# Attention, a Fourier mix and a feed-forward on one core: clears moved from the start into the first batch, mask rows loaded ahead of the identity, kept columns copied after the second stage, and the first batch's rows of maxima copied from POOL's queue

## The chip, the cores and the metric

One core of a Trainium2 chip. Its engines run side by side, each through its own instructions in order: TensorE (PE, with its weight loads PEld), VectorE (DVE), ScalarE (ACT), GpSimd (POOL) and SyncE (SP), which here only issues transfers. ACT and POOL issue transfers too, and all transfers run on the core's 16 DMA engines. The metric is device time in microseconds (us) of one execution; lower is better.

## The reference, cut to what matters

Attention over 8 batches of 8 heads, 576 positions of 64 numbers, with a mask in blocks of 64; then a real part of a two-dimensional Fourier transform of each batch's 576 x 512 result, a normalization, and a feed-forward of 512 to 2048 to 512.

```
scores = scale * np.matmul(q, k.transpose(0, 1, 3, 2))
scores = np.where(mask, scores, -1000000000.0)
scores = scores - np.max(scores, axis=-1, keepdims=True)
attn = np.exp(scores)
attn = attn / (np.sum(attn, axis=-1, keepdims=True) + 1e-09)
x = np.matmul(attn, v)            # heads side by side: (8, 576, 512)
X = np.fft.fft(np.fft.fft(x, axis=1), axis=2)
u = x + np.real(X)
un = (u - mu) / np.sqrt(var + 1e-06)
return u + np.maximum(un @ w_ch1, 0.0) @ w_ch2
```

## The kernel before

**Precision.** Products are made of two halves, a rounded high part and the rest as a low part, so most matmuls come in threes: high by high, low by high, high by low. The names show it: `ph` and `pl` are the two halves of the probabilities `p`, `VH` and `VL` of the values, `uh`/`ul` of the normalized rows, `gh`/`gl` of the hidden layer. POOL makes `pl` from `p` and `ph`, for every piece of every head.

**One head.** `lead` holds queries and keys' high parts, nine further rows for the mask, and `rest` the low parts; both are filled by copies on the chip. PE makes the maxima (`max_part`, four pieces, matmuls of `lead` alone with 72 rows), DVE reduces them into `M`, PE turns `M` by `ident` (`shift`), ACT makes the row `mt` from it, and a DMA puts `mt` into the last row of `lead`. Only then can PE make the head's `scores` (four pieces; the matmul of `lead` with 73 rows needs that row). ACT evacuates each piece twice (`ph` and `p`), POOL makes `pl`, and PE makes the values (`values`, 45 matmuls into `av`), which DVE divides by the sums. With each pair of heads the result goes to DRAM (`xd`).

**One batch.** After eight heads `mirror` reads `xd` back in two orders, into tiles and into `X2`, `U2` for the odd rows. DVE and ACT fold them (`folded`), `stage1` multiplies with tables `dft`, `stage2_sin` and `stage2_cos` do the other direction. A few columns of `stage1`'s result of two batches are kept in `ZP` (`zpc`, `zps`) and `ZTP` (`ztp`), 33 or 32 columns for each batch, since their rows are done for two batches together: `second_stage(2)` reads them after every odd batch. Rows and columns that nobody writes must be zero; that is what the clears are for. Then come the normalization and the feed (`first`, `second`; matmuls `h<-uh,W` and `acc<-W,gh`): two feeds for each batch and one more for every four batches.

**Weights.** 18 loads of 1 or 0.5 MB bring the feed's weights, issued by ACT (`weight_load`); DVE takes each apart in three passes, ACT squares it for a scale (`left`), and the first layer's low halves are made on PE (`W<-W,turns`) after the first batch's attention.

**What sets the order.** Each engine's order is written once, ahead of the run, by a planner. Work is cut into `Step`s with a chain of costs such as `("A0.26", "B", "Q0.6", "M0.05", "L1.6")`: A, D, G stand for time on ACT, DVE and POOL, P for POOL issuing a transfer, Q for SP issuing one, M for the transfer, L for its latency, B frees a PSUM bank. A step has keys that it waits for and a `place`, about the number of the head. From these the planner books queues, and takes the step that is ready with the lowest place; feed matmuls fill in where no other step is ready. A changed cost of one step so moves many instructions after it. DMA issues stand in the order of the engine that issues them.

**Lines that the change touches.** Line 255: the load of `ident`, POOL's first transfer. Lines 307 to 326: clears of `MAIN`, `DIAG` (start values of maxima), `X2`, `U2` on POOL, the loads of the masks' nine rows into the two `lead` tiles of heads 0 and 1 behind them, and clears of `ZTP` and `ZP` on DVE. `shift`: the copy of `mt` by SP. `stage1` and `stage1_tail`: ACT's copies of the kept columns at their ends. `table_lane`: four loads of `dft` by POOL, after heads 1, 2, 4 and 5.

Of the kernel before, what the change touches and what calls it, by code (L numbers as in the profile page):

```python
# [9 lines left out]
F32 = mybir.dt.float32  # L10
# [3 lines left out]
AF = mybir.ActivationFunctionType  # L14
# [18 lines left out]
HF = 2  # L33
# [186 lines left out]
def tile_attn_fourier_ffn(  # L220
# [31 lines left out]


    ident_r = const.tile([P, P], F32R, name="ident")
    gpsimd.dma_start(ident_r, c_id)
    ident = ident_r.bitcast(F32)
    rows = const.tile([P, 3], I32, name="rows")
    sync.dma_start(rows, c_rows)
# [32 lines left out]
    def both(h):  # L291

        return half_tiles(h % NB)[0:2]
# [10 lines left out]
    VH = [const.tile([P, 5, 2, D + 1], F16, name=f"VH_{i}") for i in range(2)]  # L304
    VL = [const.tile([P, 5, 2, D], F16, name=f"VL_{i}") for i in range(2)]
    ZT = const.tile([P, NCOS], F32R, name="ZT")
    for i in range(2):
        gpsimd.memset(MAIN[i], LEAST)
        gpsimd.memset(MAIN[i][0:64, 0:1], 0.0)
        gpsimd.memset(DIAG[i], LEAST)  # L310
    X2, U2 = (const.tile([P, DM], F32, name=x) for x in ("X2", "U2"))
    gpsimd.memset(X2, 0.0)
    gpsimd.memset(U2, 0.0)
    ZP = {(name, m): const.tile([P, 2, width], F32R, name=f"zp{name}{m}") for name, width in (("c", 98), ("s", 96)) for m in range(2)}
    ZTP = const.tile([P, 98], F32R, name="ztp")
    for i in range(HF):
        gpsimd.dma_start(LEAD[i][D:KS], c_masks)
        vector.tensor_scalar(LEAD[i][0:D, 0:64], ones[0:D, 0:64], 0.0, None, op0=ALU.mult)
    for i in range(2):
        vector.memset(VH[i][:, 0:4, :, D:D + 1], 1.0)  # L320
        vector.memset(VH[i][0:64, 4, :, D:D + 1], 0.0)
        vector.memset(VH[i][64:128, 4, :, D:D + 1], 1.0)
    vector.tensor_scalar(ZTP, ones[:, 0:98], 0.0, None, op0=ALU.mult)
    for t in ZP.values():
        for x in range(2):
            vector.tensor_scalar(t[:, x], ones[:, 0:t.shape[2]], 0.0, None, op0=ALU.mult)
    for at in range(0, NCOS, P):
        w = min(P, NCOS - at)
        vector.tensor_scalar(ZT[:, at:at + w], ones[:, 0:w], 0.0, None, op0=ALU.mult)
# [387 lines left out]
    def shift(h):  # L717

        t = ps_tile()
        mm(t[0:5, 0:P], M[h % 4][:, 0:5], ident_r, start=True, stop=True)  # L720
        yield
        if h >= HF:
            mt = work.tile([5, P], F32, name="mt", bufs=2).bitcast(F16)[:, 0:P]
            c = 2.0 ** -15
            scalar.activation(mt, t[0:5, 0:P], AF.Copy, bias=float(8.0 * PSHIFT * np.log(2.0)) * c, scale=-c)
            yield
            sync.dma_start(both(h)[0][KM:KS, 0:640].rearrange("r (j p) -> r j p", j=5), mt)
            yield
            return
        mt = work.tile([5, P], F32R, name="mt", bufs=2)  # L730
        scalar.activation(mt, t[0:5, 0:P], AF.Copy, bias=float(8.0 * PSHIFT * np.log(2.0)), scale=-1.0)
        yield
        dst = LEAD[h % NB][KM:KS, 0:640].rearrange("r (j p) -> r j p", j=5)
        sync.dma_start(dst.bitcast(F32), mt.bitcast(F32))
        yield

    probs = {}
# [102 lines left out]
    def max_lane():  # L840
        for h in range(2 * GP):
            for n in range(4):
                yield Step(
                    lambda n=n: max_part(h, n), 0.03 + sum(x[2] - x[1] for x in MAXPARTS[n]) / 2400.0, (f"D{(0.65, 0.49, 0.63, 0.93)[n]}",),
                    (("T", h),), ("M", h) if n == 3 else None, True, place=h - 0.6,
                )
            yield Step(lambda: shift(h), 0.12, ("A0.26", "B", "Q0.6", "M0.05", "L1.6"), (("M", h),), ("X", h), True, place=h - 0.6)
        for g in range(GP, B * H // 2):
            for n in range(4):
                d = f"D{(0.78, 0.42, 0.56, 0.91)[n]}"  # L850
                yield Step(
                    lambda n=n: pair_max(g, n), 0.06 + sum(x[2] - x[1] for x in PAIRPARTS[n]) / 2400.0, (d, "B", d),
                    (("hi", g),), ("M", 2 * g) if n == 3 else None, 2, place=2 * g - 1.6,
                )
            for h in (2 * g, 2 * g + 1):
                yield Step(
                    lambda: shift(h), 0.12, ("A0.26", "B", "Q0.6", "M0.05", "L1.6"), (("M", 2 * g), ("T", h)), ("X", h), True, place=h - 0.6
                )

    def value_lane():  # L860
# [12 lines left out]
    def fourier_steps(b):  # L873
# [69 lines left out]
        def stage1(name, m):  # L943
            mat, stack, k2, n = MATS[name]
            f0, f1, f2 = (fs[name, c] for c in range(3))
            ds = slice(P * m, P * (m + 1))
            t = ps_tile()
            i = 0
            for c, f in enumerate((f0, f1)):
                for a, w in ((0, 0), (1, 0), (0, 1)):  # L950
                    mm(t[:, 0:n], f[:, a, ds], mat[:, c, w], start=(i == 0), stop=False)
                    i += 1
            mm(t[:, 0:n], f2[0:k2, ds], stack[0:k2], start=False, stop=True)
            yield
            zz = z[name, m] = ztile(name, m).rearrange("p (x n) -> p x n", x=2)
            scalar.copy(zz[:, 0], t[:, 0:n])
            yield
            vector.tensor_tensor(zz[:, 1], t[:, 0:n], zz[:, 0].bitcast(F32), op=ALU.subtract)
            yield
            w = 33 if name == "c" else 32  # L960
            scalar.copy(ZP[name, m][:, :, o:o + w], zz[:, :, 256:256 + w].bitcast(F32))
            yield

        def stage1_tail():
            mat, stack, k2, n = MATS["c"]
            f0, f1, f2 = (fs["c", c] for c in range(3))
            t = ps_tile()
            i = 0
            for c, f in enumerate((f0, f1)):
                for w in range(2):  # L970
                    mm(t[0:2, 0:n], f[:, :, LDH], mat[:, c, w], start=(i == 0), stop=False, skip_group_check=True)
                    i += 1
            mm(t[0:1, 0:n], f2[0:k2, LDH:LDH + 1], stack[0:k2], start=False, stop=True, skip_group_check=True)
            yield
            scalar.copy(ZT[0:2], t[0:2, 0:n])
            yield
            vector.tensor_tensor(ZT[32:34], t[0:2, 0:n], ZT[0:2].bitcast(F32), op=ALU.subtract)
            yield
            scalar.copy(ZTP[:, o:o + 33], ZT[:, 256:289].bitcast(F32))
            yield  # L980

        bss = {}
# [4 lines left out]
        def stage2_sin(c):  # L987
            n = 128 if c < 2 else 96
            t = ps_tile()
            i = 0  # L990
            ns = slice(P * c, P * c + n)
            for m in range(2):
                for a, w in ((0, 0), (0, 1), (1, 0)):
                    lhs = z["s", m][:, a, ns] if c < 2 else last("s", m, a)
                    mm(t[0:n, 0:KCOL], lhs, sd[:, m, w], start=(i == 0), stop=(i == 5))
                    i += 1
            yield
            bs = bss[c] = work.tile([P, KCOL], F32, name="bs", bufs=1)
            if c == 2:
                gpsimd.memset(bs[96:97], 0.0)  # L1000
            scalar.copy(bs[0:n], t[0:n, 0:KCOL])
            yield

        def stage2_cos(c):
# [27 lines left out]
        D_ = lambda *a: ("d", b) + a  # L1032
        place = H * (b + 0.9)
        yield Step(
            mirror, 0.0, ("L3.0", "P3", "L2.5"), (("V", H * b + H - 1, 4),) + ((("F", feed_number(b - 2, 1)),) if b > 1 else ()), D_("u"),
            place=place,
        )
        def folds(name, op, width):
# [6 lines left out]
        def stages(name):  # L1045
            for m in range(2):
                yield Step(
                    lambda m=m: stage1(name, m), 0.87, ("A0.42", "D0.47", "A0.25"), (D_("f" + name),),
                    D_("z" + name) if m == 1 else None, True, place=place,
                )  # L1050
            if name == "c":
                yield Step(stage1_tail, 0.62, ("A0.4", "D0.46", "A0.23"), (D_("fc"),), D_("zt"), True, place=place)

        cos, sin = ("c", ALU.add, 257), ("s", ALU.subtract, 256)
        order = (folds(*cos), folds(*sin), stages("c"), stages("s"))
        for steps in order:
            yield from steps
        def second_stage(c):
            yield Step(lambda: stage2_sin(c), 0.67, ("A0.38",), (D_("zs"),), D_("b", c), True, place=place)
            yield Step(  # L1060
                lambda: stage2_cos(c), 0.78, ("D0.86", "B", "G3.0"), (D_("zc"), D_("zt"), D_("b", c)) + ((("F", feed_number(3, 2)),) if c == 2 and b == 5 else ()), D_("u", c), True,
                place=place,
            )

        for c in range(2):
            yield from second_stage(c)
        uu = tuple(D_("u", c) for c in range(3))
        yield from normalized_steps(low, uu[0:2], (store(b, 0), store(b, 1)), place)
        if b % 2:
# [84 lines left out]
    def feed_number(b, i):  # L1154

        return 2 * b + 1 + b // 4 + i
# [435 lines left out]
    def load_table(i):  # L1592
# [5 lines left out]
        gpsimd.dma_start(dft[:, lo:hi], c_dft[:, lo:hi])  # L1598
        yield

    def table_lane():
        for i in range(4):
            yield Step(lambda: load_table(i), 0.0, ("D0.15", "P1.0", "M2.3"), (("V", TABLES[i], 4),), ("dft", i), place=TABLES[i])

    def transform_lane():
# [114 lines left out]
```

## Time and profile before

| | us |
|---|---|
| median of 3 runs (1205.13 to 1212.7) | 1207.31 |
| the profiled execution | 1204.48 |
| its span, first to last instruction | 1202.3 |

Mean granted PE clock over the span: 0.965. By 40 slices of the span, each digit tenths:

```profile
PE   4767799998789999999999999999999999999998
PEclk9956989999889999999999999999999999999999
DMA  9687233443444234543435422360122021011100
```

A slice is 30 us. PE's row is busy share, the next its granted clock, the third the DMA engines' busy share. The first batch's attention takes the first three slices; from the 13th on PE is full.

How to read the rows of the next parts. A row of the order of time starts with its start and its length in us, then the engine, the line (L213 and L246 are helpers that record nearly every operation, so names of tiles tell more than lines), the operation, out<-in with tile names without numbers, the shape, xN where N equal ones were merged, and in brackets the idle time of its engine just before it and what ended that. SPq, ACTq are the issuing side of SP and ACT; a transfer that POOL issues is shown under POOL. Of DMA queues, q1 is SP's, q10 ACT's and q0 POOL's; a row has packets, MB and the time that the packets took as a share of 16 engines in the stretch asked for. A transfer's row shows when it was issued, not when it landed; landing is seen where somebody waits for it, or in the queue's row of a stretch.

### The profile page before, as it was taken

To read this page: it belongs to the slowest core of one execution; us is meant where nothing else is said; L and a number is where in the kernel's file an instruction comes from. 1 tells how busy PE (TensorE), PEld (TensorE's weight loads), DVE (VectorE), ACT (ScalarE), POOL (GpSimd) and SP (SyncE) were. 2 spreads that over 40 slices of the span, in tenths; PEclk is the share of its full clock that TensorE was granted. 3 is DMA by queue.
4 is the path that set the end of the run, shared out by engine and by line. 5 is a ranking of instruction groups with operands and counts; after the bars stand their busy time and mean duration, and the time that the engine had idled before them with its cause. 6 is when DMAs were issued, how large, how long until landed. Compare 5 with 4: busy or idle time off the path is not lost.

```text
span 1202.3 us, 26143 instructions
## 1 busy us (share of the span) xinstructions
PE 1122.9 (93%) x10182; PEld 824.4 (69%) x10182; DVE 741.8 (62%) x1616; ACT 630.8 (52%) x1374; POOL 475.6 (40%) x621
## 2 busy tenths in 40 slices
PE   4767799998789999999999999999999999999998
PEld 3544475675566777777776767677766766888875
DVE  6886876557857576666665566666656434454431
ACT  5666759757756566556574654675222212334320
POOL 4552414544653254425442533353334210455410
PEclk9956989999889999999999999999999999999999
DMA  9687233443444234543435422360122021011100
GB/s 259 194 253 233 105 106 87 121 124 103 123 115 103 76 87 106 113 132 81 123 99 142 126 82 82 91 151 14 32 43 56 23 60 30 28 36 26 28 19 18
DMA packets 94049, 115.07 MB, mean 96 GB/s; under 512 B 37591, under 2 KB 64129, under 8 KB 93926
## 3 DMA queue, kind: packets, MB, share of 16 engines
q1 hardware_dynamic: 86582, 89.06, 28.2%
q10 hardware_dynamic: 4384, 16.78, 4.3%
q0 software_dynamic: 2960, 7.58, 2.3%
q8 instruction: 80, 1.31, 0.5%
q14 instruction: 43, 0.35, 0.1%
HBM read 58.50 MB, written 18.89 MB: 64 GB/s over the span
## 4 chain that ended last, share of the span: by engine, by line
PE 70%; DVE 1%; DMA 1%; ACT 0%; SPq 0%; issue 0%; POOL 0%; DVEq 0%; ACTq 0%; POOLq 0%
PE acc L246 24%; PE ps L246 23%; PE h L246 17%; PE av L246 6%; DMA lead<-mt 1%; DMA rest<-lead 0%; SPq L213 0%; DVE p L213 0%; PE ps L249 0%; DVE M L213 0%; DVE gl L213 0%; ACT p L213 0%; DVE st L213 0%; DVE x L213 0%; PE h L249 0%
## 5 line engine op out<-in xcount | busy, mean ns | idle before, releaser
L213 POOL TENSOR_TENSOR pl<-p,ph 128x288 f16<-128x288 f32 (+1 forms) x256 | 261.0, 1029 | 345.6 <-ACT ph L213 188.3
L246 PEld LDWEIGHTS <-W 128*128 128x128 f16 x3456 | 332.5, 98 | 60.4 <-issue 1.5
L246 PE MATMUL acc<-W,gh 128*128 128x512 f16 (+1 forms) x1008 | 289.5, 369 | 1.5 <-DVE W L213 1.2
L246 PE MATMUL ps<-uh,W 128*128 128x256 f16 x1184 | 217.6, 273 | 0.0
L246 PE MATMUL h<-uh,W 128*128 128x256 f16 x1120 | 207.7, 275 | 0.0
L246 PE MATMUL acc<-W,gl 128*128 128x512 f16 (+1 forms) x504 | 186.2, 370 | 1.0 <-DVE gl L213 1.0
L246 PE MATMUL ps<-ul,W 128*128 128x256 f16 x592 | 161.2, 272 | 0.0
L246 PE MATMUL h<-ul,W 128*128 128x256 f16 x560 | 153.8, 275 | 0.1
L246 PEld LDWEIGHTS <-ph 128*128 128x128 f16 x2112 | 132.4, 102 | 27.1 <-issue 4.6
L246 PEld LDWEIGHTS <-gh 128*128 128x128 f16 x1056 | 98.8, 98 | 69.5 <-issue 1.8
L246 PE MATMUL av<-VH,pl 128*128 128x65 f16 (+1 forms) x963 | 117.2, 201 | 19.1 <-POOL pl L213 16.4
L213 DVE TENSOR_REDUCE M<-ps 128x1 fp32r<-128x320 f32 (+4 forms) x214 | 96.1, 483 | 59.7 <-PE ps L246 53.9
L246 PE MATMUL ps<-lead 73*128 73x288 f16 (+10 forms) x494 | 115.9, 295 | 14.1 <-DMA lead<-in_c_masks_dram 10.3
L246 PE MATMUL av<-VH,ph 128*128 128x65 f16 (+1 forms) x966 | 119.2, 202 | 3.2 <-DVE x L213 2.6
L246 PEld LDWEIGHTS <-pl 128*128 128x128 f16 x1056 | 102.9, 101 | 24.4 <-POOL pl L213 20.4
L246 PE MATMUL av<-VL,ph 128*128 128x64 f16 x960 | 117.4, 200 | 0.0
L213 ACT ACTIVATE gh<-ps 128x512 f16<-128x512 f32 x74 | 44.0, 594 | 114.8 <-PE ps L246 114.8
L213 ACT CAST ph<-p 128x512 f16<-128x512 f32 (+1 forms) x188 | 98.3, 523 | 5.1
L213 DVE SCALAR_TENSOR_TENSOR gl<-ps,gh 128x512 f16<-128x512 f32 x74 | 50.8, 688 | 80.3 <-ACT gh L213 79.9
L213 ACT ACTIVATE p<-ps 128x288 f32<-128x288 f32 (+1 forms) x159 | 79.4, 500 | 30.1 <-PE ps L246 26.5
L246 PEld LDWEIGHTS <-gl 128*128 128x128 f16 x528 | 51.5, 98 | 58.9 <-DVE gl L213 2.4
L246 PEld LDWEIGHTS <-lead 73*128 73x128 f16 (+1 forms) x744 | 64.9, 103 | 34.5 <-issue 6.1
(295 smaller groups left out, 1948.8 us busy)
## 6 DMA issues: line engine op xcount, KB each, us to landing
raw<-in_qk_dram SPq DMA_DIRECT2D x30, 576.0 KB
W<-in_moe_w_ch_dram ACTq DMA_DIRECT2D x14, 1024.0 KB
V<-in_v_dram SPq DMA_DIRECT2D x32, 320.0 KB
rest<-lead SPq DMA_DIRECT2D x64, 144.0 KB
rest<-rest SPq DMA_DIRECT2D x60, 144.0 KB
out_dram<-u SPq DMA_DIRECT2D x32, 256.0 KB
xd<-x SPq DMA_DIRECT2D x30, 256.0 KB
lead<-lead SPq DMA_DIRECT2D x60, 72.0 KB
```

The lines of the kernel that those rows point to most:

```text
L213: x = f(*args, **kw)
L246: return tc.keep_in_program_order(nc.tensor.matmul(*args, **kw))
```

## The change

- POOL's first transfers are now the masks' rows for heads 0 and 1, then `ident`; before, `ident` came first and the masks after eight clears.
- `X2`, `U2` (POOL), `ZTP` and `ZP` (nine instructions, DVE before, ACT now) are no longer cleared at the start, but in a new step `clear`, after head 4.
- The kept columns are copied by ACT in a new step `save`, after the second stage's first two parts, and not at the ends of `stage1` and `stage1_tail`. The first two batches' `mirror` waits for `clear`; `second_stage(2)` waits for `save`.
- For heads 0 to 7 the copy of `mt` into `lead` is issued by POOL, not SP, and the planner books 1.0 us of POOL for it in place of 0.6 us of SP.

```diff
@@ start
-    gpsimd.dma_start(ident_r, c_id)
...
+    for i in range(HF):
+        gpsimd.dma_start(LEAD[i][D:KS], c_masks)
+    gpsimd.dma_start(ident_r, c_id)
     for i in range(2):
         gpsimd.memset(MAIN[i], LEAST)
...
-    gpsimd.memset(X2, 0.0)
-    gpsimd.memset(U2, 0.0)
...
     for i in range(HF):
-        gpsimd.dma_start(LEAD[i][D:KS], c_masks)
         vector.tensor_scalar(LEAD[i][0:D, 0:64], ones[0:D, 0:64], 0.0, None, op0=ALU.mult)
...
-    vector.tensor_scalar(ZTP, ones[:, 0:98], 0.0, None, op0=ALU.mult)
-    for t in ZP.values():
-        for x in range(2):
-            vector.tensor_scalar(t[:, x], ones[:, 0:t.shape[2]], 0.0, None, op0=ALU.mult)
@@ shift
-            sync.dma_start(both(h)[0][KM:KS, 0:640].rearrange("r (j p) -> r j p", j=5), mt)
+            (gpsimd if 0 <= h < 8 else sync).dma_start(both(h)[0][KM:KS, 0:640].rearrange("r (j p) -> r j p", j=5), mt)
...
-        sync.dma_start(dst.bitcast(F32), mt.bitcast(F32))
+        (gpsimd if 0 <= h < 8 else sync).dma_start(dst.bitcast(F32), mt.bitcast(F32))
@@ max_lane
-            yield Step(lambda: shift(h), 0.12, ("A0.26", "B", "Q0.6", "M0.05", "L1.6"), (("M", h),), ("X", h), True, place=h - 0.6)
+            yield Step(lambda: shift(h), 0.12, ("A0.26", "B", "P1.0" if 0 <= h < 8 else "Q0.6", "M0.05", "L1.6"), (("M", h),), ("X", h), True, place=h - 0.6)
@@ stage1, stage1_tail
-            w = 33 if name == "c" else 32
-            scalar.copy(ZP[name, m][:, :, o:o + w], zz[:, :, 256:256 + w].bitcast(F32))
-            yield
...
-            scalar.copy(ZTP[:, o:o + 33], ZT[:, 256:289].bitcast(F32))
@@ fourier_steps
-            mirror, 0.0, ("L3.0", "P3", "L2.5"), (("V", H * b + H - 1, 4),) + ((("F", feed_number(b - 2, 1)),) if b > 1 else ()), D_("u"),
+            mirror, 0.0, ("L3.0", "P3", "L2.5"), (("V", H * b + H - 1, 4),) + ((("F", feed_number(b - 2, 1)),) if b > 1 else (("clear",),)), D_("u"),
...
-                    lambda m=m: stage1(name, m), 0.87, ("A0.42", "D0.47", "A0.25"), (D_("f" + name),),
+                    lambda m=m: stage1(name, m), 0.87, ("A0.42", "D0.47"), (D_("f" + name),),
...
+        def save():
+            for name, w in (("c", 33), ("s", 32)):
+                for m in range(2):
+                    scalar.copy(ZP[name, m][:, :, o:o + w], z[name, m][:, :, 256:256 + w].bitcast(F32))
+            scalar.copy(ZTP[:, o:o + 33], ZT[:, 256:289].bitcast(F32))
+            yield
...
         for c in range(2):
             yield from second_stage(c)
+        yield Step(save, 0.0, ("A1.25",), (D_("zs"), D_("zc"), D_("zt"), ("clear",)), D_("save"), place=place)
@@ table_lane
+    def clear():
+        gpsimd.memset(X2, 0.0)
+        gpsimd.memset(U2, 0.0)
+        scalar.activation(ZTP, ones[:, 0:98], AF.Copy, scale=0.0)
+        for t in ZP.values():
+            for x in range(2):
+                scalar.activation(t[:, x], ones[:, 0:t.shape[2]], AF.Copy, scale=0.0)
+        yield
...
         for i in range(4):
+            if i == 3:
+                yield Step(clear, 0.0, ("A2.2",), (("V", TABLES[i] - 1, 4),), ("clear",), place=TABLES[i] - 1)
```

**What moves, 1: POOL's start.** POOL's row from its first transfer on; `lead_93`, `lead_94` are heads 0 and 1 (`lead_92`, `lead_93` after). Before:

```order
L213 DMA ident<-in_c_id_dram 128x128
L213 MEMSET MAIN_101 128x5
L213 MEMSET MAIN_101 64x1
L213 MEMSET DIAG_103 128x5
L213 MEMSET MAIN_102 128x5
L213 MEMSET MAIN_102 64x1
L213 MEMSET DIAG_104 128x5
L213 MEMSET X_118 128x512
L213 MEMSET U_119 128x512
L213 DMA lead_93<-in_c_masks_dram 9x1216
L213 DMA lead_94<-in_c_masks_dram 9x1216
```

And now:

```order
L213 DMA lead_92<-in_c_masks_dram 9x1216
L213 DMA lead_93<-in_c_masks_dram 9x1216
L213 DMA ident<-in_c_id_dram 128x128
L213 MEMSET MAIN_100 128x5
L213 MEMSET MAIN_100 64x1
```

The first copies of `mt`, further down POOL's row, now:

```order
L213 TENSOR_TENSOR rest_95<-raw,lead_93 64x576
L213 DMA lead_92<-mt 1x5x128
L213 DMA lead_93<-mt 1x5x128
L213 MEMSET ul 128x1
L213 TENSOR_TENSOR pl_254<-p_280,ph_253 128x288
```

The masks' two loads now come ahead of `ident`; the copies of `mt` for heads 0 and 1 stand behind the last subtraction for `rest` and ahead of the first `pl`. Those of heads 2, 3 and 4 stand behind the last `pl` of the head before, head 5's right behind head 4's; head 6's, and then the clears of `X2` and `U2`, stand ahead of the last `pl` of head 5.

**What moves, 2: ACT around head 3's row of maxima.** `ph_...` and `p_...` are evacuations of head 2's scores, `W<-` a weight load. Before:

```order
L213 ACTIVATE ph_525<-ps_527 128x512
L213 ACTIVATE mt<-acc 5x128
L213 ACTIVATE p_572<-ps_527 128x512
L213 ACTIVATE ph_534<-ps_536 128x512
L213 ACTIVATE p_594<-ps_536 128x512
L213 DMA W<-in_moe_w_ch_dram 128x2x1024
```

Now:

```order
L213 ACTIVATE mt<-acc 5x128
L213 ACTIVATE p_557<-ps_523 128x288
L213 ACTIVATE ph_526<-ps_528 128x512
L213 ACTIVATE ph_538<-ps_540 128x512
L213 ACTIVATE p_574<-ps_528 128x512
L213 ACTIVATE p_582<-ps_540 128x512
L213 ACTIVATE lead_517,vacc<-raw 128x576
L213 ACTIVATE rest_518,vacc<-raw 128x576
L213 DMA W<-in_moe_w_ch_dram 128x2x1024
```

The weight load stood four rows behind `mt`, and stands eight behind it now.

**What moves, 3: PE where the second transform begins.** `acc<-W,g..` are the second feed's second layer, `dft` matmuls the transform. Before, the second feed's last group is followed by scores, and the transform's first matmul comes 300 rows later, behind values:

```order
L246 MATMUL acc<-W,gh 128x512
L246 LDWEIGHTS gl
L246 MATMUL acc<-W,gl 128x512
L246 LDWEIGHTS rest_547
L246 MATMUL h_3882<-rest_547 128x448
L246 LDWEIGHTS lead_546
```

Now the feed's last group stands between two parts of the transform:

```order
L246 MATMUL acc<-W,gl 128x512
L246 MATMUL ps_3860<-dft,fs_3582 128x290 x3
L246 MATMUL ps_3860<-dft,fs_3653 128x290 x3
L246 MATMUL ps_3860<-dft,fs_3559 128x290
L246 LDWEIGHTS gh
L246 MATMUL acc<-W,gh 128x512
L246 LDWEIGHTS gh
L246 MATMUL acc<-W,gh 128x512
L246 LDWEIGHTS gl
L246 MATMUL acc<-W,gl 128x512
L246 MATMUL h_3879<-dft,fs_3582 128x290 x3
```

The transform has moved ahead of the end of the second feed. From the second feed's last matmul to the third feed's first there were 424 matmuls (62,060 columns), and there are 271 (43,142 columns).

More of the change, by code (lines that the diff above doesn't have):

```diff
@@ L856, in max_lane @@
                 yield Step(
-                    lambda: shift(h), 0.12, ("A0.26", "B", "Q0.6", "M0.05", "L1.6"), (("M", 2 * g), ("T", h)), ("X", h), True, place=h - 0.6
+                    lambda: shift(h), 0.12, ("A0.26", "B", "P1.0" if 0 <= h < 8 else "Q0.6", "M0.05", "L1.6"), (("M", 2 * g), ("T", h)), ("X", h), True, place=h - 0.6
                 )
@@ L977, in stage1_tail @@
             vector.tensor_tensor(ZT[32:34], t[0:2, 0:n], ZT[0:2].bitcast(F32), op=ALU.subtract)
-            yield
-            scalar.copy(ZTP[:, o:o + 33], ZT[:, 256:289].bitcast(F32))
             yield
@@ L1051, in stages @@
             if name == "c":
-                yield Step(stage1_tail, 0.62, ("A0.4", "D0.46", "A0.23"), (D_("fc"),), D_("zt"), True, place=place)
+                yield Step(stage1_tail, 0.62, ("A0.4", "D0.46"), (D_("fc"),), D_("zt"), True, place=place)
         cos, sin = ("c", ALU.add, 257), ("s", ALU.subtract, 256)
@@ L1058, in second_stage @@
         def second_stage(c):
-            yield Step(lambda: stage2_sin(c), 0.67, ("A0.38",), (D_("zs"),), D_("b", c), True, place=place)
+            yield Step(lambda: stage2_sin(c), 0.67, ("A0.38",), (D_("zs"),) + ((D_("save"),) if c == 2 else ()), D_("b", c), True, place=place)
             yield Step(
```

## The prediction, made before the changed kernel ran

> **What bounds the kernel now.** I read the page first (busy shares, the slices), then the busy time by stretches, then what PE waited for, then the order of time at the places of the change. All of it is one execution of 1204.48 us, span 1202.3; the median of the three runs shown, 1207.31, is 2.83 above it.
>
> ```profile
> PE 1122.9 (93%) x10182; PEld 824.4 (69%) x10182; DVE 741.8 (62%) x1616; ACT 630.8 (52%) x1374; POOL 475.6 (40%) x621
> 0.00:40.00 40.00, 21.14 (x139) 17.33 (x140) 28.42 (x79) 21.84 (x46) 18.38 (x30) 1.00 0.78 225
> 40.00:80.00 40.00, 29.85 (x282) 20.53 (x280) 35.09 (x67) 25.23 (x61) 19.91 (x24) 0.71 0.84 255
> 80.00:120.00 40.00, 26.78 (x157) 15.84 (x155) 28.65 (x62) 25.91 (x55) 14.74 (x19) 0.67 0.71 224
> 360.00:400.00 40.00, 40.00 (x393) 27.82 (x392) 27.99 (x63) 24.56 (x53) 14.61 (x17) 1.00 0.37 92
> ```
>
> The columns of a stretch are PE, weight loads, DVE, ACT, POOL, PE's granted clock, DMA share, GB/s. From 360 us on PE is full at clock 1.00. The matmuls are the same ones before and after the change, so the time can change only by what PE idles, or runs at a lower clock, ahead of 360 us. There DMA is at 0.71 to 0.84 and DVE at 28 to 35 of 40 us: three resources share the first 120 us.
>
> ```profile
> PE av L246 <- POOL pl L213: 12.5, 16, 1.9
> PE ps L246 <- DMA lead<-in_c_masks_dram: 10.3, 1, 10.3
> PE acc L246 <- DMA lead<-mt: 8.2, 4, 2.7
> ```
>
> These are PE's longest waits up to 250 us (us, times, longest). The change touches the second and third, and puts work on POOL, the releaser of the first.
>
> **Start: masks first.**
>
> ```profile
> 1.26 0.80 POOL L213 DMA_DIRECT2D ident<-in_c_id_dram  x1 [0.82 <-POOLq L1702]
> 2.65 0.53 POOL L213 MEMSET X<- 128x512 f32 x1
> 3.12 0.52 POOL L213 MEMSET U<- 128x512 f32 x1
> 3.59 1.06 POOL L213 DMA_DIRECT2D lead<-in_c_masks_dram  x2
> 5.07 1.15 ACT L213 CAST lead<-raw 64x1152 fp32r<-64x1152 f32 x1 [3.06 <-DMA raw<-in_qk_dram]
> 10.34 1.62 PE L246 MATMUL ps<-lead 72*128 72x64 f32 x5 [10.34 <-DMA lead<-in_c_masks_dram]
> 12.87 0.38 ACTq L213 DMA_DIRECT2D W<-in_moe_w_ch_dram  x1
> 15.83 0.86 SPq L213 DMA_DIRECT2D lead<-mt  x1
> 20.53 0.61 PE L246 MATMUL acc<-lead 73*128 73x288 f32 x1 [1.76 <-DMA lead<-mt]
> q10 hardware_dynamic: 270, 1.04, 75.4%
> ```
>
> The masks' copies are issued at 3.59, after the identity and the clears, and land at 10.3. Issued at 1.26 instead, ahead of most loads, they leave the cast of raw (ends 6.22) as the last input: PE starts its first maxima 4.1 us earlier. But PE's next stop is the score of head 0 at 20.53, on the copy of the row of maxima. The last row shows what stood before that copy: from 16 to 20 us a 1 MB weight load (issued 12.87) moved, and the copy issued at 15.83 landed only behind it. The change brings that load's issue forward too (it waits for DVE behind the same maxima), so it still stands ahead of the copy, and the bytes ahead of the copy are the same. DMA is the limit here (0.78 of the whole stretch). Gain between 0 and 1.76 + 4.1 = 5.9 us; I take 0.5, near the lower end, because the row of 16 to 20 us is this very copy's. The two clears that leave POOL (0.53 + 0.52) and the nine that leave DVE stood ahead of the first landing (5.07), where both engines wait for loads anyway: 0.
>
> **Rows of maxima through POOL.** Where was a copy late?
>
> ```profile
> 43.20 0.27 ACT L213 ACTIVATE mt<-acc 5x128 f16<-5x128 f32 x1 [0.36 <-PE acc L246]
> 43.21 0.37 ACTq L213 DMA_DIRECT2D W<-in_moe_w_ch_dram  x1
> 43.93 0.75 SPq L213 DMA_DIRECT2D lead<-mt  x1
> 49.61 0.40 PE L246 MATMUL acc<-lead 73*128 73x288 f16 x1 [2.69 <-DMA lead<-mt]
> 69.84 0.40 PE L246 MATMUL acc<-lead 73*128 73x288 f16 x1 [2.33 <-DMA lead<-mt]
> 39.65 0.40 PE L246 MATMUL acc<-lead 73*128 73x288 f16 x1 [1.39 <-DMA lead<-mt]
> q10 hardware_dynamic: 243, 0.97, 80.8%
> ```
>
> Head 3: ACT makes mt at 43.20, and at 43.21 its queue issues a weight load that stands four rows behind mt; SP's copy goes out at 43.93. From 45 to 48 us (last row) the load moves 0.97 MB, and PE waits till 49.61. SP is 0.5 us late, the load 3 us: the queue that issues the copy isn't what makes it late. Does POOL's queue pass such a load? The nearest rows are its own small copies:
>
> ```profile
> 110.15 0.37 ACTq L213 DMA_DIRECT2D W<-in_moe_w_ch_dram  x1
> 111.63 1.11 POOL L213 DMA_DIRECT2D fs<-add  x2 [5.23 <-ACT add L213]
> 117.94 0.58 PE L246 MATMUL h<-dft,fs 98*128 98x290 f32 x1 [2.95 <-DMA fs<-add]
> q0 software_dynamic: 64, 0.00, 2.2%
> ```
>
> Two 1 KB copies issued on POOL at 111.63, 1.5 us after a weight load, moved only between 115.5 and 117.5 (last row) and landed 6.3 us after issue. SP's copy of head 3 took 5.7. So by these rows POOL's queue is no faster behind a load: 0 for the queue itself. The Trainium skill says otherwise ("DMA: Bandwidth & Descriptors", section on queues, rings and completion order): each DMA engine takes the queue rows in turn, packet by packet. By that rule a small copy on a row of its own would pass the load, and the sum would be that of the first rival below; the POOL row above disagrees.
>
> What does help is the order, which allows 1.0 us more for this copy. For head 3, the load stood four rows behind mt on ACT and now stands eight behind, past two evacuations; PE now has the six maxima of the next head and 45 value matmuls between the shift and the score that needs it. For head 5 the copy is now made before the whole of head 4's scores. So 2.69 + 2.33 = 5.0 us of these waits should go; head 2's 1.39 stays, its load is five rows behind as before. Ends: 0 (another input is late instead) to 6.4. I take 5.0.
>
> Price on POOL: eight issues of 0.56 (the row at 111.63 has two in 1.11) are 4.5 us among subtractions that PE already waits for (12.5 us). In the order each copy stands behind the last subtraction of the head before or ahead of the first of its own head, where POOL would idle; only head 6's stands ahead of a subtraction that is due, and with it the two clears. I take 1.0 of 0 to 4.5. The clears on ACT are nine small instructions; nearest row is mt's 0.27, so 2.4 us, ahead of the maxima of head 7 and the first evacuation of head 6. I take 1.0 of 0 to 2.4. DVE, at 67.5 of the 80 us from 10 to 90 (second row below), is next to be late: 0.5. The kept columns, 0.24 each on ACT, are copied as often as before, only later, and PE's longest waits name none of them: 0.
>
> ```profile
> L213 ACT CAST zpc<-zc x16: 242/243/249, 120.0 to 1022.4; 128x66 fp32r<-128x66 f32 x16
> 10.00:90.00 80.00, 56.01 (x475) 41.72 (x476) 67.50 (x137) 48.85 (x114) 38.17 (x43) 0.81 0.79 241
> ```
>
> **Stretch without feed-forward work.**
>
> ```profile
> 284.00:340.00 56.00, 43.41 (x465) 32.74 (x464) 42.28 (x108) 41.32 (x95) 31.00 (x37) 0.88 0.45 125
> 225.00:284.00 59.00, 58.73 (x621) 42.32 (x618) 35.60 (x84) 36.81 (x83) 23.62 (x25) 1.00 0.41 115
> 287.63 0.38 PE L246 MATMUL acc<-W,gl 128*128 128x512 f16 x1
> 301.73 1.19 PE L246 MATMUL h<-dft,fs 128*128 128x290 f32 x7
> 337.84 0.27 PE L246 MATMUL h<-uh,W 128*128 128x256 f16 x1
> 356.14 0.28 PE L246 MATMUL h<-lead 73*128 73x288 f16 x1 [2.92 <-DMA lead<-mt]
> ```
>
> The second feed ends at 287.63 and the third begins at 337.84; between them PE has only attention and the second transform, idles 12.6 of the 56 us and falls to clock 0.88, where the stretch before, with feed, has 0.3 idle. In the order 424 matmuls lie between these two feed rows before, 271 after, because the transform now begins while the second feed still has groups to give. Idle shrinks by the share of columns (62,060 to 43,142, three tenths): 12.6 × 0.30 = 3.8. The lost clock is 0.12 × 43.4 = 5.2, three tenths of it 1.6. Gain 5.4, ends 0 and 10.8 (double, if the transform in between is fully covered). The wait at 356.14 is left where it is.
>
> **Sum.** -0.5 - 5.0 + 1.0 + 1.0 + 0.5 - 5.4 = -8.4 against 1204.48: 1196.1 for the profiled execution, and with 2.83 for the median 1198.9, say 1199.
>
> **Rivals.** Two more stretches bear on the third: all engines from 111.4 to 116.4, and POOL's queue from 270 to 272 us behind its own issue.
>
> ```profile
> 111.40:116.40 5.00, 1.96 (x8) 1.07 (x6) 4.31 (x9) 2.99 (x6) 1.25 (x4) 0.80 0.99 319
> 269.62 1.11 POOL L213 DMA_DIRECT2D fs<-add  x2 [4.83 <-ACT add L213]
> q0 software_dynamic: 64, 0.00, 1.9%
> ```
>
> 1. POOL's queue does pass the loads. For it: a queue of its own. Against: the rows of 110 to 118 us. Then head 0's copy lands early (5.4 more) and head 2's wait goes (1.4): 1199 - 6.8 = 1192. With these gaps gone the clock too would hold between 40 and 120 us, where 0.31 of 56.6 busy us is at most 17.5 us; a third of that makes 1186. Chance 0.22.
> 2. The waits only change their name. DVE's 67.5 of 80 us stay, and PE's waits for pl are larger than those for mt; the gain of 5.0 is then taken by them, and the shorter stretch gives only half: 1199 + 5.0 + 2.7 = 1207, no change. Chance 0.24.
> 3. Slower: POOL's copies land late by themselves. The rows at 111.63 leave open whether the weight load or DVE held them, since DVE was busy for 4.31 of the 5 us from 111.4. If DVE does, each of the four heads that wait loses up to 5.2 us more (from 112.7, when POOL was done, to 117.9), 20.8 in all, and the 5.0 doesn't come: 1225. Without the 5.0 there are 3.4 us left to lose, so it decides from 0.85 us per copy. Against it: at 269.62 the same two copies moved within 2.4 us of the issue. Chance 0.09. The Trainium skill ("SBUF — State Buffer", section "SBUF: two separate sides") has such a trap: the descriptors of a DMA from POOL can't be written while DVE holds the port that the two share. By it the loss would be of this rival's size; no row here shows a case that only it explains.
>
> **How the numbers follow.** My forecast, 1199 with its own range of 1193 to 1206, has 0.45. About 1% is what a measurement of this kernel can tell from no change: faster means below 1195.2, slower above 1219.4. Faster: 0.20 from rival 1 and 0.17 from the lower part of the forecast and a fuller stretch, 0.37. Slower: rival 3, 0.09. The rest, 0.54, lies within 1%. The range goes from rival 1 with a third of the clock, 1186, to 1214, which is the forecast without its two large gains (+10.4) and with POOL's and ACT's prices at their upper ends (+4.9).
>
> **What would show each step.** PE's first matmul at about 6.3 us, and the first score still near 20 us (well under 18 speaks for rival 1). No wait on mt at heads 3 and 5, one at head 2 and at head 0. The waits for pl up to 250 us no more than 14 us. Transform matmuls of the second batch before the second feed's last group, and under 10 us of idle where 12.6 was. PE full after that. The forecast is wrong if PE idles anew behind head 6 (the clears), if the copies on POOL take over 6 us with no load ahead of them, or if the new order opens a gap after 360 us.

## The result, and the profile after

The changed kernel takes 1215.76 us (median of 20 runs, 1211.05 to 1222.14), the kernel before 1206.93 (20 runs, 1203.25 to 1214.22). The ratio is 1.0063, 95% interval 1.005 to 1.0076: slower by 0.6%, where 1199 and a gain were forecast. The profiled execution took 1216.2 us, its span is 1214.4, 12.1 more than before's.

First the line of busy times on the page of the changed kernel, then its busy time by stretches (columns as before: PE, weight loads, DVE, ACT, POOL, PE's granted clock, DMA share, GB/s):

```profile
PE 1123.9 (93%) x10182; PEld 823.8 (68%) x10182; DVE 741.5 (61%) x1607; ACT 629.9 (52%) x1383; POOL 482.9 (40%) x629
```

```profile
0.00:40.00 40.00, 23.73 (x159) 18.99 (x160) 29.70 (x77) 23.53 (x49) 19.97 (x32) 1.00 0.77 228
40.00:120.00 80.00, 49.96 (x402) 31.93 (x400) 57.11 (x115) 48.20 (x112) 35.68 (x50) 0.82 0.73 224
120.00:284.00 164.00, 144.26 (x1298) 100.42 (x1298) 112.42 (x247) 111.26 (x246) 66.72 (x71) 0.94 0.38 109
284.00:360.00 76.00, 68.26 (x710) 51.62 (x709) 56.50 (x129) 51.48 (x120) 42.76 (x50) 0.93 0.36 99
360.00:720.00 360.00, 352.00 (x3513) 254.98 (x3511) 232.73 (x538) 212.09 (x473) 142.32 (x163) 0.99 0.39 103
720.00:1190.00 470.00, 466.65 (x3987) 353.93 (x3985) 249.57 (x499) 181.56 (x383) 175.42 (x264) 1.00 0.21 53
```

The same cuts of the kernel before, where they were not shown:

```profile
40.00:120.00 80.00, 56.62 (x437) 36.37 (x435) 63.74 (x128) 51.13 (x115) 34.65 (x43) 0.69 0.78 240
120.00:284.00 164.00, 148.43 (x1379) 102.76 (x1379) 113.94 (x247) 114.72 (x254) 68.41 (x75) 0.95 0.37 104
284.00:360.00 76.00, 60.50 (x645) 45.79 (x644) 55.11 (x135) 52.12 (x119) 42.38 (x52) 0.89 0.45 124
360.00:720.00 360.00, 360.00 (x3620) 260.99 (x3619) 235.54 (x551) 218.51 (x483) 144.83 (x168) 1.00 0.40 105
720.00:1190.00 470.00, 469.25 (x3935) 357.48 (x3934) 242.98 (x475) 171.89 (x359) 166.96 (x254) 1.00 0.19 47
```

PE is busy for 1123.9 us, 1.0 more than before, so the time is in what it idles. Stretch length minus PE's busy time, after against before: 16.3 against 18.9 (0 to 40 us), 30.0 against 23.4 (40 to 120), 19.7 against 15.6 (120 to 284), 7.7 against 15.5 (284 to 360), 8.0 against 0.0 (360 to 720), 3.4 against 0.8 (720 to 1190). Two stretches gain 10.4 us together, the four others lose 21.4; with PE's 1.0 us these are the 12.1. The cuts lie at fixed times, so the same stretch doesn't hold quite the same work: the transform behind the first batch's attention begins at 119.97 us, where it began at 112.95. The start and the stretch without feed-forward work came out better, as forecast; the rest of the first batch, and the part where PE used to be full, came out worse.

What PE waited for in the changed kernel up to 250 us (us, times, longest; beside these 6.5 us are the start itself):

```profile
PE ps L246 <- DMA lead<-mt: 10.6, 2, 5.9
PE av L246 <- POOL pl L213: 10.1, 14, 2.0
PE acc L246 <- DMA lead<-mt: 3.9, 3, 2.3
```

The waits for rows of maxima are 14.5 us where 8.2 stood, and two of them make 10.6. The first is head 3's. In order of time, all engines:

```profile
40.83 0.27 ACT L213 ACTIVATE mt<-acc 5x128 f16<-5x128 f32 x1 [1.28 <-PE acc L246]
41.62 0.34 SPq L213 DMA_DIRECT2D raw<-in_qk_dram  x1
...
45.30 0.60 SPq L213 DMA_DIRECT2D rest<-lead  x1
...
53.36 0.40 PE L246 MATMUL ps<-lead 73*128 73x288 f16 x1 [4.67 <-DMA lead<-mt]
```

And POOL's own row in these microseconds, with the issue of the copy at 47.05:

```profile
42.89 2.12 POOL L213 TENSOR_TENSOR pl<-p,ph 128x512 f16<-128x512 f32 x1 [0.70 <-ACT p L213]
...
45.06 2.05 POOL L213 TENSOR_TENSOR pl<-p,ph 128x512 f16<-128x512 f32 x1
47.05 0.53 POOL L213 DMA_DIRECT2D lead<-mt  x1
...
54.59 0.72 POOL L213 TENSOR_TENSOR pl<-p,ph 128x288 f16<-128x288 f32 x1 [6.42 <-ACT p L213]
```

ACT had mt at 41.10; POOL issued the copy 5.95 us later, behind two subtractions of 2.1 us, and by then SP had issued seven transfers (raw to rest, 41.62 to 45.30) that fill the next heads' tiles, and ACT a weight load (at 42.48). POOL stood idle for 0.70 us just ahead of the first of these subtractions, with mt ready: an issue of 0.53 us would have fitted there. In the stretch from issue to landing:

```profile
q10 hardware_dynamic: 272, 1.05, 40.4%
q1 hardware_dynamic: 518, 0.84, 34.0%
...
lead<-mt POOLq DMA_DIRECT2D x1, 1.2 KB, 6.3
```

(From 45 to 53.4 us: packets, MB, share of 16 engines; last row KB and us to landing.) Before, the copy went out 0.5 us after mt, and SP's fills came behind it. The second long wait, head 4's:

```profile
56.09 0.27 ACT L213 ACTIVATE mt<-acc 5x128 f16<-5x128 f32 x1 [1.28 <-PE acc L246]
59.70 0.37 ACTq L213 DMA_DIRECT2D W<-in_moe_w_ch_dram  x1
59.89 0.57 POOL L213 DMA_DIRECT2D dft<-in_c_dft_dram  x1
60.45 1.05 POOL L213 DMA_DIRECT2D lead<-mt  x2
67.41 0.40 PE L246 MATMUL ps<-lead 73*128 73x288 f16 x1 [5.90 <-DMA lead<-mt]
```

It too is issued 4 us after mt, behind a weight load and behind a load of dft on POOL's own queue.

### The profile page after: what moved, and what is told of

It is laid out like the page before. It is cut to its first block, busy times and chain, and to the rows that moved or that the text cites. A ratio compares the mean times of both kernels' runs of the same rounds, so it can differ in the third digit from the quotient of the medians.

```text
span 1214.4 us, 26143 instructions
## 1 busy us (share of the span) xinstructions
PE 1123.9 (93%) x10182; PEld 823.8 (68%) x10182; DVE 741.5 (61%) x1607; ACT 629.9 (52%) x1383; POOL 482.9 (40%) x629
## 4 chain that ended last, share of the span: by engine, by line
PE 77%; DVE 7%; DMA 5%; POOL 4%; ACT 3%; issue 2%; SPq 1%; DVEq 0%; POOLq 0%; ACTq 0%
PE acc L246 26%; PE ps L246 25%; PE h L246 19%; PE av L246 7%; DMA lead<-mt 2%; DVE W L213 2%; DVE M L213 2%; POOL pl L213 2%; DMA lead<-rest 1%; SPq L213 1%; POOL ag L213 1%; POOL x L213 1%; ACT ph L213 1%; DVE un L213 1%; ACT p L213 1%
## 5 line engine op out<-in xcount | busy, mean ns | idle before, releaser
L246 PE MATMUL ps<-uh,W 128*128 128x256 f16 x1232 | 228.1, 273 | 0.4 <-DVE gl L213 0.4
L246 PE MATMUL h<-uh,W 128*128 128x256 f16 x1072 | 198.2, 275 | 0.5 <-DVE M L213 0.5
L246 PE MATMUL ps<-ul,W 128*128 128x256 f16 x616 | 168.2, 273 | 0.0
L246 PE MATMUL h<-ul,W 128*128 128x256 f16 x536 | 147.3, 275 | 0.0
L246 PE MATMUL ps<-lead 72*128 72x64 f16 (+11 forms) x484 | 113.2, 296 | 23.9 <-DMA lead<-mt 13.2
L213 DVE TENSOR_REDUCE M<-ps 128x1 fp32r<-128x448 f32 (+4 forms) x200 | 90.7, 488 | 49.5 <-PE ps L246 48.9
```

Source lines behind the costliest of these rows:

```text
L213: x = f(*args, **kw)
L246: return tc.keep_in_program_order(nc.tensor.matmul(*args, **kw))
```

## The experiments

All ratios are to the kernel before as it ran in the same five rounds (medians 1207.25 to 1208.38 us), with 95% intervals. Each profile is of one execution, up to 4.2 us off the median of its kernel. "PE's order" is the sequence of its matmuls in the program, tile numbers left out.

### Who issues the copy, and what the planner books for it

Two theories at first: POOL as issuer is late (A), or the new order loses the time (B). The four kernels take the issuer and the booked cost apart.

**SP issues, the changed order kept.**

```
-(gpsimd if 0 <= h < 8 else sync).dma_start(...mt)      # both places in shift
+sync.dma_start(...mt)
```

> The changed kernel with one thing undone: SP issues the rows of maxima again, while every other engine keeps the changed order (the planner still books 1.0 us of POOL). Theory A, POOL's own order makes the copies late: in the changed kernel POOL issued the copies of heads 2, 3 and 4 at 36.45, 47.05 and 60.45, 4.7, 6.0 and 4.1 us after ACT had made mt, because they stand behind subtractions, and the scores of heads 3 and 4 then waited 4.67 and 5.90 us. With SP issuing within 1 us of mt, each of these two waits falls to 1 to 2 us, so 6 to 9 us come back: 0.993 to 0.995 of the changed kernel, 0.999 to 1.001 of the kernel before. Rival B, the order itself (the new steps move matmuls and evacuations, and gaps open at 160 to 240 us and after 360 us): the two waits only change their releaser, the time stays at 1.005 to 1.008 of the kernel before.

Measured: 1216.78 us, 1.0076 (1.0054 to 1.0097). SP does no better, so the loss isn't that of POOL as issuer alone. But SP didn't issue within 1 us of mt either, as the expectation had assumed. Its row shows why:

```profile
41.04 0.27 ACT L213 ACTIVATE mt<-acc 5x128 f16<-5x128 f32 x1 [1.28 <-PE acc L246]
...
53.39 0.74 SPq L213 DMA_DIRECT2D lead<-mt  x1
55.45 0.40 PE L246 MATMUL ps<-lead 73*128 73x288 f16 x1 [7.23 <-DMA lead<-mt]
```

The copy goes out 12 us after mt. In the program it stands behind the seven transfers that fill the next heads' tiles, and waits for ACT, which was long done, and for a semaphore that ACT's weight load, issued at 43.28, raises too. That load moves 0.11 MB between 50 and 52 us and nothing after. So SP's copy, 6.7 us behind the last of the fills (46.07, 0.59 long), was, as far as these rows show, held by the weight load. The copy's place in the order is late for either issuer.

**POOL issues, booked as before.**

```
-"P1.0" if 0 <= h < 8 else "Q0.6"                        # both places in max_lane
+"Q0.6"
```

> The changed kernel, but the planner books the old 0.6 us of SP for the copy, so that the order is that of the clears and kept columns alone; POOL still issues the eight copies. Theory A (POOL issues them late): it stands 4 to 9 us above the same order with SP issuing, with waits on mt of 3 us and more in the first 100 us. Rival B (order): no more than 2 us from the same order with SP issuing.

Measured: 1197.95 us, 0.9927 (0.9907 to 0.9947).

**The rest of the change alone**: both edits above, so SP issues and is booked.

> The change without its part on the rows of maxima: SP issues and is booked as before; masks first, late clears and late kept columns stay. Theory A: the loss is gone and the earlier start (2.5 us at the first score) stays: 0.996 to 1.000 of the kernel before. Rival B, the order that the new steps bring loses the time: 1.004 to 1.008 of the kernel before.

Measured: 1197.45 us, 0.9927 (0.9901 to 0.9954). These two differ by 0.5 us. So the issuer is worth nothing that these runs can tell, in either order, and the cost that the planner books, with the same matmuls and the same transfers, is worth 16 to 18 us (0.9927 against 1.0063, 1197.95 against 1215.76). Head 3 when POOL issues from the early place (ACT makes mt at 40.38):

```profile
40.94 0.53 POOL L213 DMA_DIRECT2D lead<-mt  x1 [0.85 <-ACT mt L213]
...
46.24 0.40 PE L246 MATMUL acc<-lead 73*128 73x288 f16 x1 [2.14 <-DMA lead<-mt]
```

**The rows of maxima alone, on the kernel before**: POOL issues and is booked 1.0 us, nothing else is changed.

> The kernel before with the part on the rows of maxima alone: POOL issues the eight copies and is booked 1.0 us for each; clears, masks and kept columns as before. PE's order of the kernel before stays nearly as it was. Theory A: copies of heads 2 to 5 go out 2 to 6 us after mt, two or three scores wait 4 to 6 us for them instead of 1.4 to 2.7, and the time is 1.004 to 1.009 of the kernel before. Rival B: within 0.002 of the kernel before, since its order is kept.

Measured: 1216.32 us, 1.0074 (1.0053 to 1.0095). The size fits A; what has fallen of A is the issuer, not the late copy. Behind the first 6% of PE's rows its order is the one of before, so what makes the loss lies in the first batch's rows. Scores there wait 4.96 and 6.22 us for mt, and the first transform begins at 123.00 us in place of 112.95: 10 of the 15 us between the two profiled executions.

### The copy's place, with PE's order held

New theory (C): the planner books the issue on POOL's own timeline, where it must find a free slot of 1.0 us among the subtractions; it finds one only behind them, so the copy is written late, behind the fills. Rival (D): PE's new order loses the time by itself. To hold PE, ACT and DVE row for row, the copy is written in one piece with mt, for all heads, whatever is booked:

```
 scalar.activation(mt, ...)
-yield
 sync.dma_start(...mt)            # and once more with gpsimd for h < 8, below
```

> The changed kernel with the order of PE, ACT and DVE kept row for row, but each copy of a row of maxima is written directly behind ACT's mt, and SP issues it for all heads. For head 3 it so stands ahead of the seven transfers that fill the next heads' tiles, not behind them. Theory C, the place of the copy behind these transfers makes the score late: the wait of head 3's score (4.67 us in the changed kernel, 7.23 us with SP issuing behind the fills) falls to 0 to 2 us, and 3 to 6 us come back: 0.995 to 0.998 of the changed kernel, 1.001 to 1.005 of the kernel before. Rival D, the order of PE's own matmuls (scores behind the next head's maxima) loses the time: PE waits elsewhere instead, and the time stays at 1.005 to 1.008 of the kernel before.

Measured: 1206.97 us, 0.9997 (0.9976 to 1.0018), 9 us below the changed kernel and 10 below the run with SP issuing behind the fills, more than was expected. In the order of time:

```profile
40.68 0.27 ACT L213 ACTIVATE mt<-acc 5x128 f16<-5x128 f32 x1 [1.28 <-PE acc L246]
41.69 0.75 SPq L213 DMA_DIRECT2D lead<-mt  x1
...
64.65 0.24 PE L246 MATMUL av<-VH,pl 128*128 128x65 f16 x1 [4.30 <-POOL pl L213]
```

The copy now goes out 0.7 us after mt, ahead of the fills (the first at 42.54), and no score but head 0's waits for a copy in the first 110 us. Some of it comes back as a wait for pl, 4.3 us.

**The same place, POOL issues.**

> The changed kernel with the order of PE, ACT and DVE kept row for row and POOL issuing, but each copy of a row of maxima is written directly behind ACT's mt, ahead of the subtractions and of the transfers that fill the next heads' tiles. Theory C, the copy's place alone made the changed kernel slower: 0.990 to 0.995 of the changed kernel, 0.996 to 1.002 of the kernel before, as with SP issuing from that place (0.9997). Rival, POOL as the issuer costs by itself (subtractions wait behind a copy that waits for ACT): 1.004 of the kernel before or more.

Measured: 1203.52 us, 0.9949 (0.9922 to 0.9976), 12 us below the changed kernel, again more than was expected, and again POOL as issuer costs nothing (it is 3.4 us ahead of SP from the same place, with intervals that touch). The two profiled executions, with the same order on PE, are 9.7 us apart at the end. The first batch's attention makes 8.1: the transform behind it starts at 111.89 here and at 119.97 in the changed kernel. At 360 us 3.8 of these are left (the same matmul at 356.29 and 360.07). The rest comes behind 575 us, where the edit moved copies of later heads too; a wait of 2.68 us for one at 586.99 is gone. So C holds, an early copy gains; what the first batch's eight are worth of the 12 us isn't separated from the later ones. D isn't ruled out: with early copies the changed order is still behind the order booked with 0.6 us of SP, 0.9949 against 0.9927 with POOL issuing, where the intervals overlap, and 0.9997 against 0.9927 with SP, where they don't.

**The same 1.0 us, booked on SP.** POOL issues.

```
-"P1.0" if 0 <= h < 8 else "Q0.6"
+"Q1.0" if 0 <= h < 8 else "Q0.6"
```

> The changed kernel, POOL issuing the eight copies, but the planner books 1.0 us of SP for each in place of 1.0 us of POOL. Theory C (the planner finds no gap of 1.0 us among POOL's subtractions, so it writes the copy and the score late; the size alone does nothing): PE's order is nearly that of the run booked with 0.6 us of SP, and the time is 0.990 to 0.996 of the kernel before. Rival (a longer booking of any engine moves the order): 1.004 to 1.008.

Measured: 1198.96 us, 0.9916 (0.9886 to 0.9946). So 1.0 us does no harm on SP's timeline and does on POOL's. The trace shows that POOL's issue takes 0.53 us, half of what was booked. Smaller bookings on POOL were not timed. By the order alone, with 0.6 us the copies stand where they do with SP booked, while 0.7 already puts head 2's behind two subtractions. It isn't only the size: 0.5 puts those of heads 4 and 5 behind the last subtraction of the head before again.

### The other parts, one by one

**Masks first, alone** (the two masks' loads moved ahead of `ident`).

> The kernel before with the masks' rows issued first on POOL and nothing else changed; every order but the start of POOL's is that of the kernel before. PE's first maxima start at about 6.3 us instead of 10.34. If the copy of the first row of maxima still stands behind a weight load that was issued earlier too, the first score stays near 20 us (19.8 to 20.5) and the time is 0.998 to 1.001 of the kernel before. If the start is carried through, the first score comes at 16 to 18 us and the time falls by 2.5 to 4 us, 0.996 to 0.998.

Measured: 1207.16 us, 0.9978 (0.9955 to 1.0001). The first score comes at 19.99, after a wait of 4.27 us for its copy, so the first case holds; the time fits both. At the end of the first batch the profile is 2.5 us ahead of the kernel before (the same matmul at 127.68 and 130.18), and by 310 us it is level (310.04 and 310.05).

**Late clears, alone** (the clears moved into `clear`, kept columns as before).

> The kernel before with the clears of X2, U2, ZTP and ZP moved behind the fifth head and nothing else changed; PE's order is that of the kernel before. By the prediction's price (the clears at the start were hidden, the late ones cost about 1 us on ACT): 1.000 to 1.002 of the kernel before. If the clears at the start were in the way of the first loads' users: 0.995 to 0.998.

Measured: 1205.32 us, 0.9977 (0.9956 to 0.9998): a small gain at most, no price.

**Masks and late clears.**

> The kernel before with the masks' rows issued first and the clears moved behind the fifth head, kept columns copied as before; PE's order is that of the kernel before. If the clears at the start held DVE and POOL back once the masks come first: 0.991 to 0.995 of the kernel before. If not: 0.997 to 1.000, as with the masks alone (0.9978).

Measured: 1206.0 us, 0.9976 (0.9957 to 0.9995): the two don't add.

**Kept columns later, alone** (`save` in place of the copies in `stage1`, clears at the start).

> The kernel before with the kept columns copied in their own later step and nothing else changed (clears and masks at the start as before). PE's order is then that of the run without the part on the rows of maxima (1197.45 us), which differs from the kernel before from the first transform on. If that order is where the gain of 0.7% comes from: 0.991 to 0.997 of the kernel before, with 47 to 48 us of busy PE between 284 and 340 us where it had 43.4. If the gain came from the start (masks, clears): 0.999 to 1.002.

Measured: 1206.68 us, 0.9991 (0.9973 to 1.0009). Nothing that can be told, though PE's order is that of the 1197.45 us run and PE is busy for 48.3 us between 284 and 340, about as the first case had it.

**Masks first and kept columns later.**

> The kernel before with the masks' rows issued first and the kept columns copied later, clears at the start as before; PE's order is that of the run that had all but the part on the rows of maxima (1197.45 us). If the parts only add (masks -2.6 us, kept columns -1.1): 0.996 to 0.998 of the kernel before, and the late clears make the rest. If the new order needs the earlier start: 0.991 to 0.994.

Measured: 1199.21 us, 0.9917 (0.9888 to 0.9946). So these two make nearly the whole gain together, and next to none apart. Over the same matmuls the two profiles are still level at 300 us (300.94 with the kept columns alone, 300.83 with the masks first too); the lead opens later, in steps, to 3.1 us at 360 and 8.8 at the end. One of the steps, PE's longest wait from 470 to 560 us, kept columns alone and then with the masks first:

```profile
483.07 0.44 PE L246 MATMUL ps<-lead 72*128 72x64 f16 x4 [2.67 <-DMA lead<-rest]
```

```profile
479.26 0.44 PE L246 MATMUL ps<-lead 72*128 72x64 f16 x4 [1.65 <-DMA lead<-rest]
```

Here the lead is 3.8 us, and 5.4 by 490 us, since the granted clock fell behind the first of these waits (0.50 from 484 to 486) and not behind the second (1.00 from 478 to 484; more in the last section). What makes the two parts worth 8 us together stays open.

## Why the prediction was wrong, step by step

**Rows of maxima through POOL, -5.0: this step failed.** The prediction said "the queue that issues the copy isn't what makes it late", which the runs bear out: with the order held, POOL and SP are 0.5 us apart (1197.95, 1197.45) and 1.0 (1215.76, 1216.78), and POOL ahead by 3.4 at most. It then said "What does help is the order, which allows 1.0 us more for this copy", and read from rows on ACT and PE that more work stood between mt and the score. It did: PE had work until 48.69, 7.6 us past mt (with 3.1 us of waits for pl in it), where it had 3.4 before (43.47 to 46.92). But the copy itself was put behind two subtractions on POOL and behind SP's fills, 5.95 us later. The row of the copy on POOL was read, and taken for one "where POOL would idle"; it idled because of it, 6.42 us for the next evacuation, since that hangs on the score that waits for the copy. The waits went from 8.2 to 14.5 us in place of 3.2. The runs price the place of the copy at 10 us with SP issuing (1216.78 to 1206.97) and 12 with POOL (1215.76 to 1203.52), copies of later heads included, and with SP the wait for a weight load. Ahead of the first transform alone it is 5.1 us (119.04 to 113.95) and 8.1, and 10 where the part is put on the kernel before (112.95 to 123.00).

**POOL's price, +1.0.** The waits for pl up to 250 us fell from 12.5 to 10.1 us, so the price doesn't show there. The cost ran the other way: the copy was late behind the subtractions.

**Start, -0.5.** With the masks alone the first score came at 19.99 instead of 20.53, as said. In the changed kernel it came at 18.00, 2.5 us earlier, because POOL's first copy landed sooner than SP's (last section). The step was right for the masks. For the pair it was 2 us too small at the first score, but that lead doesn't last: of two kernels that differ in the issuer alone, the one with POOL makes the first score at 17.97, the other at 19.83, and 5 us later they are level (23.15 and 23.27).

**Clears, +1.0, and DVE, +0.5.** Moving the clears alone gained 0.2% (0.9956 to 0.9998), so a gain of up to 0.4% in place of a loss; beside the masks it adds nothing (0.9976 against 0.9978). No run separates the 0.5 for DVE.

**Stretch without feed, -5.4.** Right for the stretch, not for the time. Between the second feed's last matmul and the third's first, before and after:

```profile
288.01:337.84 49.83, 37.79 (x428) 29.07 (x426) 37.34 (x97) 37.51 (x87) 28.42 (x33) 0.86 0.42 116
295.89:329.90 34.01, 26.55 (x274) 20.86 (x273) 26.70 (x62) 23.96 (x59) 20.19 (x25) 0.85 0.43 120
```

PE idles 7.5 us where it idled 12.0, and the clock takes 0.15 of 26.6 busy us in place of 0.14 of 37.8, 1.3 us less: 5.8 us. But with the kept columns alone PE idles 5.5 us there (291.01 to 316.85) and the kernel is no faster (0.9991). So a gain in this stretch isn't by itself a gain of the kernel.

**"From 360 us on PE is full."** This premise failed: 8.0 us of idle from 360 to 720 and 2.6 us more behind. The changed kernel's longest waits behind 420 us:

```profile
PE ps L246 <- DMA lead<-mt: 2.7, 1, 2.7
PE acc L246 <- DVE gl L213: 2.2, 1, 2.2
PE h L246 <- DMA lead<-rest: 2.2, 1, 2.2
```

Such gaps are no property of the late copies alone. The run without that part has them too (5.5 us from 360 to 720, from a single profile) and is still 0.7% faster; masks alone, with the transform's old order, has 4.4, most of it one wait of 3.88 us for a copy that ends at 490.34. So that work spent ahead of 360 us is missing later is one reading, and not shown.

**The rivals.** The first, POOL's queue passes the loads, holds at the start only and is worth 3.4 us at most in the time, with intervals that touch. The second, waits that change their name, is seen where the copies come early: 4.3 us for pl at 64.65. The third has the sign; in time (1225) it is 9 us off, as the second (1207) is on the other side. Its sign comes for another reason: the copies didn't move slower from POOL, they were issued late. The rule of the Trainium skill beside it ("SBUF — State Buffer", section "SBUF: two separate sides") isn't needed: with POOL issuing the eight copies, 1197.95 us shows no such loss. What no rival had is that one booked cost moves the copy against the transfers on SP.

Without the late place the change lands where the forecast was (1199): booked on SP it takes 1197.95 (0.6 us) or 1198.96 (1.0 us), and both beat both kernels. It doesn't get there by the forecast's terms, though: the waits for rows of maxima are 8.5 us in the first, as many as before.

## What to carry to other kernels

When a plan decides the order, a booked cost is a change to the program: read the moved instruction's place on its own queue against everything that now stands ahead of it there and on the other queues, and hold the booking against the measured time (0.53 us here, 1.0 booked). That a booking nearer to the measured time gives a better order isn't shown. A small transfer that the critical path waits for belongs directly behind what makes it, ahead of the bulk transfers; who issues it mattered far less here. Parts of a change can be worth 0.1% and 0.2% alone and 0.8% together, so test them together as well as one by one.

## What the runs showed of the hardware beyond that

A wait of 2.7 us on a PE that is otherwise full can cost more than its length. In the changed kernel, around the wait of 2.68 us that ends at 586.99 (columns as above, the clock is the third from the right):

```profile
586.00:588.00 2.00, 1.01 (x5) 0.69 (x5) 0.00 (x0) 0.49 (x2) 0.00 (x0) 0.67 0.01 4
588.00:590.00 2.00, 2.00 (x10) 1.24 (x9) 0.00 (x0) 1.28 (x4) 1.45 (x2) 0.50 0.00 0
```

PE is busy again from 586.99, but up to 590 at half its clock: 3 us of which half is lost, beside the 2.68. The length of the wait doesn't decide it. With SP issuing and the same order on PE, the same matmul waits 2.69 us, until 587.25, and the clock stays:

```profile
586.00:588.00 2.00, 0.75 (x7) 0.63 (x7) 0.00 (x0) 0.37 (x1) 0.00 (x0) 1.00 0.02 8
588.00:590.00 2.00, 2.00 (x18) 1.22 (x16) 0.20 (x1) 1.94 (x6) 1.37 (x2) 1.00 0.00 0
```

A later wait of 2.24 us for gl goes the other way round in these two kernels: the clock stays at 1.00 in the changed one (912 to 916 us) and falls to 0.57 with SP issuing (907 to 909). What decides isn't shown here. A page of the Trainium skill ("TensorE: Matmul & The Clock Gate", section "Part 1: The HAM clock gate") puts the fall after an idle window of about 3.4 us; here waits of 2.24 and 2.68 us were followed by one.

At one place a small copy from POOL passed part of a weight load. With the same order on PE, POOL's first copy was issued later than SP's and landed sooner; POOL issuing first, then SP:

```profile
12.44 0.54 POOL L213 DMA_DIRECT2D lead<-mt  x1 [0.96 <-ACT mt L213]
...
17.97 0.61 PE L246 MATMUL acc<-lead 73*128 73x288 f32 x1 [2.00 <-DMA lead<-mt]
```

```profile
11.75 0.86 SPq L213 DMA_DIRECT2D lead<-mt  x1
...
19.83 0.61 PE L246 MATMUL acc<-lead 73*128 73x288 f32 x1 [4.49 <-DMA lead<-mt]
```

5.5 us against 8.1 from issue to the score. With POOL issuing, ACT's queue moved 1.69 MB from 9 to 16.5 us; a load has 1.05 MB, so what follows is still its second, issued at 8.95. The queues from 16.5 to 17.2 us (first two rows) and from 17.2 to 18.4:

```profile
q10 hardware_dynamic: 36, 0.15, 73.2%
q0 software_dynamic: 32, 0.00, 4.2%
...
q10 hardware_dynamic: 59, 0.24, 65.8%
```

POOL's copy moved (q0) while 0.24 MB of the load were still to come. Of the three pairs that differ in the issuer alone, two show nothing of it in the time (0.5 and 1.0 us), and the third 3.4 us with intervals that touch.
